# Moving the weight-sum transfer chains of an attention and two feed-forward stages out of the attention, with a shorter ring of weight buffers

## The chip, the cores and the metric

One core of one Trainium2 chip. The metric is device time in microseconds (us) of one execution. Of the kernel before there are three runs: 1626.64, 1627.64 and 1628.63 us.

## What is computed

```python
def reference(**kwargs):
    attn_out = _attn_ref(**attn_kwargs)          # 2 x 8 heads, 768 x 64; scores masked to equal cluster
    B, H, S, D = attn_out.shape
    x = np.ascontiguousarray(attn_out.transpose(0, 2, 1, 3)).reshape(B * S, H * D)
    x = _moe_ref(x=x, **moe_kwargs)              # softplus(x @ w_in) @ w_out, 512 -> 2048 -> 512
    return _moe2_ref(x=x, **moe2_kwargs)         # 8 experts: out += P[:, e] * (relu(x @ w1[e]) @ w2[e])
```

`P` comes from a gate, an exponential and eight rounds of normalising rows and columns. There are 1536 tokens in two batches of 768.

## The kernel before

The program has three stages on one core. **Attention** walks through eight pairs of heads; for each it loads q, k and v, splits each float32 operand into a rounded high part and a low part (`HL`), finds the cluster of each row (`sm`, `tp`, `A`, `OH`), copies rows into the score operands by DMA (`AT`, `Bt`, lines 372 and 451), and does scores (`s`, line 498), exponentials (`E`), transposes (`t`, line 538), the split of the transposed tile (`eh` on ACT, `el` on DVE, line 545) and the product with v (`av`). **The first feed-forward stage** has 16 entries (eight chunks of the hidden width, two batches, list `m1`), each of seven steps; its weights arrive as 64-bit numbers (`r`, lines 139 and 143), are turned into float32 by DVE (`to32`, lines 123 to 127) and split (`wh`, `wl`, `w2h`, `w2l`). **The expert stage** has 16 blocks `k` (two batches, eight experts), each of two layers (`l1_group`, line 910; `l2_piece`, line 945) that use a Strassen-like scheme with seven products in place of eight.

That scheme needs sums of quarters of each expert's two weight matrices. They don't depend on the data, so DMA makes them: `t_step` runs a **chain** of ten transfers for one matrix. A quarter is loaded into a buffer `ts` (SP's queue, line 209), others are added onto it by a transfer that accumulates (POOL's queue, line 207), and the four sums T1 to T4 are written to DRAM (`td`, line 198). Each transfer waits for the one before it:

```python
    STEPS = ("B11", "+B12", "T1", "+B22", "T2", "+B21", "T4", "B12", "+B22", "T3")
```

A transfer that must wait holds up all that stands behind it on its queue: SP issues nearly all other loads and the copies of the attention, POOL also does subtractions and the cluster work. There are 16 chains (`JOBS`, eight experts, two matrices). `JA` and `JF` say where they run: the first four in the attention (one buffer), six in the first feed-forward stage (two buffers), six in the expert blocks (one buffer, one chain per block). Their place is given as a planned time: `at` in the attention, `tsum_at` by feed-forward entry and step, `do` in the expert blocks (28 units of time per block, list `ev2`). A tracing scheduler then makes each engine's order from these times, the priorities and the dependences; `behind_pe` only ties a step's place in that order to TensorE's.

Other names: `W2R` is a ring of four buffers for the second expert matrix (line 856), `w2_load` fills it, `w2_split` splits it on ACT (`vh`) and POOL (`vl`, line 868). `w1_split` splits the first expert matrix in chunks A and B (low part on DVE, line 840) and C (POOL). `xc_prep` (line 968) makes the sums S1 to S4 of the second batch's input (`xS`, lines 72 and 74) and splits seven operands (`chA`, `clA`, `chS`, `clS`, line 990) in the last four groups of steps of block 7. `sinkhorn` is the normalising of `P`, two phases per round, on DVE with a small product `cp` on TensorE.

Of the kernel before, what the change touches and what calls it, by code (L numbers as in the profile page):

```python
# [20 lines left out]
def attention_moe_moe2(ctx, tc, v, qt, kt, centroids, w_in, w_out, w_gate, w1, w2, eye, out, dbg=None):  # L21
# [169 lines left out]
    def t_step(pool, m, e, n):  # L191
        what = STEPS[n]
        if n == 0:
            TS[m, e] = slot_pool[pool].tile([P, 1024], F32, tag="ts", name=f"ts{m}_{e}", bufs=TSB[pool])
        t, w = TS[m, e], what.lstrip("+")
# [25 lines left out]

    TSB = {"ap": 1, "fp": 2, "gp": 1}
    JOBS = [(m, e) for e in range(E) for m in range(2)]
    JA, JF = 4, 10

# [374 lines left out]
    for n in range(4):  # L600
        at(175 + n * 5, lambda n=n: x_split("1_0", first_blk, n), ("xs", 0))
    for j, job in enumerate(JOBS[:JA]):
        for n in range(10):
            at(22 + 42 * j + 4.1 * n, lambda job=job, n=n: behind_pe(t_step, "ap", *job, n), ("tl", 0))
    KEEP = {'sp2': 1, 'fr': 0, 'av': 1, 'am3': 1, 'tpa': 1, 'smc': 0, 'm0': 1, 'rw': 1, 'pz': 1, 'e1': 1}
# [227 lines left out]
    def w1_split(k, u, ch):  # L833
        h, l = T = w1_tiles(ch, 0, f"m{k}_{u}")
        n = 0
        for src in WR[u % 2, ch]:
            m = src.shape[1]
            hs = h[:, n : n + m, :]
            nc.scalar.copy(hs, src)
            (nc.gpsimd if ch == "C" else nc.vector).tensor_tensor(l[:, n : n + m, :], src, hs.bitcast(F32), ALU.subtract)  # L840
            n += m
        W1U.setdefault((k, u), {}).update(w1_use({ch: T}))
# [11 lines left out]
    def w2_load(k, i):  # L854
        name, e = PROD[i][1], k % E
        dst = W2R[(7 * k + i) % 4]
        if name[0] == "B":
# [6 lines left out]
    def w2_split(k, i, p):  # L864
        src = W2R[(7 * k + i) % 4][:, 2 * p : 2 * p + 2, :]
        h, l = (gp.tile([P, 2, DM // 2], F32R, tag=f"v{t}", name=f"v{t}{k}_{i}{p}", bufs=4) for t in "hl")
        nc.scalar.copy(h, src)  # L867
        nc.gpsimd.tensor_tensor(l, src, h.bitcast(F32), ALU.subtract)  # L868
        WH[k, i, p] = h, l
# [97 lines left out]
    def xc_prep(sb, step):  # L967
# [9 lines left out]
        def add(name):  # L977
# [3 lines left out]
            else:  # L981
                tag = {"S1": "A22", "S2": "A12", "S3": "A21"}[name]
                t = gp.tile([P, 2, FH], F32, tag="X" + tag, name=f"x{name}{key}", bufs=XB[tag])
# [3 lines left out]
        def split(name):  # L987
            hi, lo = XC[key, name] = tiles(name)
            nc.scalar.copy(hi, blk[name])
            (nc.gpsimd if name == "A22" else nc.vector).tensor_tensor(lo, blk[name], hi.bitcast(F32), ALU.subtract)  # L990

        for name in (("A11",), ("A12",), (), ("+S1", "+S2", "S2"), ("S1", "+S3", "S3"), ("+S4", "S4"), ("A22",))[step]:
            (add if name[0] == "+" else split)(name.lstrip("+"))
# [11 lines left out]
    for k in range(NB):  # L1005
        for u in range(4):
# [6 lines left out]
            for i in range(7):  # L1013
                do(t0 + i, l1_group, k, u, i)
                if k == E - 1 and u == 3:
                    do(t0 + i + 0.9, xc_prep, 1, i)
        S0 = t1[k] + G1
# [11 lines left out]
        for i in range(7):  # L1029
            b, i_ = divmod(7 * k + i - 4, 7)  # L1030
            do(split_at[b][2 * i_ + 1] + 0.15 if b >= 0 else -1, w2_load, k, i)
# [6 lines left out]
    for j, job in enumerate(JOBS[JF:]):  # L1038
        for n in range(10):
            do(G1 * (j + 1) - 22 + 2.75 * n, behind_pe, t_step, "gp", *job, n)  # L1040
    for hf in range(2):
        do(0.5 + hf, lambda hf=hf: gate(1, hf))
        do(2.5 + 1.5 * hf, lambda hf=hf: gate_max(hf))
    for it in range(8):
        for ph in range(2):
            do(5.5 + 4 * it + 2.5 * ph, lambda it=it, ph=ph: sinkhorn(it, ph))

    tsum_at = {}
    for j, job in enumerate(JOBS[JA:JF]):
        for n in range(10):  # L1050
            tsum_at.setdefault(divmod(1 + int(14.5 * (j // 2 * 2) + 10 * (j % 2) + 2.85 * n), 7), []).append(
                lambda job=job, n=n: behind_pe(t_step, "fp", *job, n)
            )
# [78 lines left out]
```

## Time and profile before

| | |
|---|---|
| profiled execution | 1626.69 us, of which the span of its instructions is 1624.9 us |
| median of the three runs | 1627.64 us |
| TensorE (PE) busy | 1527.6 us, 94% of the span |
| VectorE (DVE) busy | 1257.0 us, 77% |
| ScalarE (ACT) busy | 1005.4 us, 62% |
| GpSimd (POOL) busy | 706.5 us, 43% |
| mean granted TensorE clock | 0.975 of full speed |
| attention | 0 to about 317.5 us |
| first feed-forward stage | about 317.5 to 610 us |
| expert blocks 0 to 7 (first batch) | about 613 to 1108 us |
| expert blocks 8 to 15 (second batch) | to the end |

A stage's engine that is busy without gaps sets that stage's time; an engine's idle time matters only where another waits for it. The stage limits above are the first matmuls of lines 654 and 910 in the trace.

### The profile page before, as it was taken

How to read it: one execution, taken by the hardware profiler on the slowest of the kernel's cores; microseconds unless marked ns; L12 is line 12 of the kernel's file. 1: busy time of each engine (PE TensorE's matmuls, PEld its weight loads, DVE VectorE, ACT ScalarE, POOL GpSimd, SP SyncE). 2: the span in 40 equal slices, each digit the busy share in tenths (PEclk: the TensorE clock that was granted, in tenths of full speed). 3: DMA queues.
4: the chain of work that ended last, by engine and by line, in shares of the span. 5: the costliest groups of instructions: out<-in, count | busy, mean ns of one | idle time of the engine just before them, and what ended most of it. 6: DMA issues, size and time to landing. Idle time of an engine off the chain costs nothing. (4 is left out here: it accounts for less than half of the span.)

```text
span 1624.9 us, 26977 instructions
## 1 busy us (share of the span) xinstructions
PE 1527.6 (94%) x9873; PEld 1449.9 (89%) x9873; DVE 1257.0 (77%) x1836; ACT 1005.4 (62%) x1854; POOL 706.5 (43%) x536
## 2 busy tenths in 40 slices
PE   5888889989999999899999999998999999999998
PEld 4777778879999977799999999998999999999998
DVE  4879779886666266878888888798878878878877
ACT  4767768766665544565665665665566666566663
POOL 3333333432323122355555555555455454445544
PEclk8989989989999999999999999999999999999999
DMA  7678776479888305767788775334443434433421
GB/s 221 167 182 214 183 167 154 98 176 252 212 222 213 101 14 137 190 182 213 202 208 212 205 206 159 121 100 120 145 129 121 124 120 127 124 121 120 125 74 66
DMA packets 268533, 253.02 MB, mean 156 GB/s; under 512 B 12272, under 2 KB 235632, under 8 KB 268400
## 3 DMA queue, kind: packets, MB, share of 16 engines
q1 hardware_dynamic: 242656, 217.67, 44.2%
q0 software_dynamic: 25600, 33.56, 13.3%
q8 instruction: 77, 1.26, 0.3%
q14 instruction: 56, 0.46, 0.1%
q10 hardware_dynamic: 144, 0.07, 0.0%
HBM read 194.10 MB, written 36.70 MB: 142 GB/s over the span
## 5 line engine op out<-in xcount | busy, mean ns | idle before, releaser
L868 POOL TENSOR_TENSOR vl<-w2r,vh 128x512 fp32r<-128x512 f32 x224 | 359.2, 1608 | 410.7 <-ACT vh L867 402.3
L889 DVE TENSOR_TENSOR gl<-XA,gh 128x768 fp32r<-128x768 f32 x160 | 180.2, 1126 | 79.0 <-ACT gh L888 79.0
L888 ACT CAST gh<-XA 128x768 fp32r<-128x768 f32 x160 | 133.9, 837 | 106.9 <-PE Ya1m L945 92.9
L207 POOL DMA_DIRECT2D ts<-in_moe_w_dram x64 | 80.8, 1270 | 193.0 <-DMA ts<-in_moe_w_dram 74.0
L945 PE MATMUL Ya0m<-vh,gl 128*128 128x256 f32 x512 | 144.3, 282 | 0.4 <-DVE gl L889 0.4
L945 PE MATMUL Ya0m<-vh,gh 128*128 128x256 f32 x512 | 144.1, 281 | 0.0
L945 PE MATMUL Ya0m<-vl,gh 128*128 128x256 f32 x512 | 144.1, 281 | 0.0
L867 ACT CAST vh<-w2r 128x512 fp32r<-128x512 f32 x224 | 137.6, 615 | 9.6 <-PE y L688 6.3
L545 DVE TENSOR_TENSOR el<-t,eh 128x384 fp32r<-128x384 f32 x192 | 102.2, 549 | 29.1 <-ACT eh L541 27.6
L541 ACT CAST eh<-t 128x384 fp32r<-128x384 f32 x192 | 90.7, 479 | 37.6 <-PE t L538 24.6
L945 PE MATMUL Yb0m<-vl,gh 128*128 128x256 f32 x384 | 109.5, 285 | 2.6 <-POOL vl L868 2.6
L506 DVE TENSOR_REDUCE sc<-s 128x1 f32<-128x768 f32 x96 | 91.2, 951 | 26.8 <-PE s L498 26.4
L538 PE MATMUL t<-idf,E 128*128 128x128 f32 x576 | 100.6, 284 | 11.9 <-DVE el L545 9.9
L945 PE MATMUL Yb0m<-vh,gh 128*128 128x256 f32 x384 | 109.2, 284 | 2.4 <-DVE x L963 2.4
L945 PE MATMUL Yb0m<-vh,gl 128*128 128x256 f32 x384 | 109.6, 285 | 1.9 <-DVE gl L889 1.9
L931 ACT ACTIVATE XA<-XA 128x768 f32<-128x768 f32 x96 | 81.3, 847 | 41.4 <-DVE XA L929 41.4
L945 PEld LDWEIGHTS Ya0m<-vh,gl 128*128 128x128 f32 x512 | 97.1, 190 | 0.6 <-DVE gl L889 0.6
L945 PEld LDWEIGHTS Ya0m<-vh,gh 128*128 128x128 f32 x512 | 96.9, 189 | 0.0
L945 PEld LDWEIGHTS Ya0m<-vl,gh 128*128 128x128 f32 x512 | 96.9, 189 | 0.0
L511 ACT ACTIVATE E<-s,sc 128x768 f32<-128x768 f32 x96 | 87.0, 906 | 15.4 <-DVE sc L506 14.1
L538 PEld LDWEIGHTS t<-idf,E 128*128 128x128 f32 x576 | 74.8, 146 | 23.7 <-DVE el L545 13.4
L72 DVE TENSOR_TENSOR XS<-XA,XA 128x768 f32<-128x768 f32 x32 | 62.4, 1949 | 33.4 <-ACT XA L927 33.4
(246 smaller groups left out, 5293.1 us busy)
## 6 DMA issues: line engine op xcount, KB each, us to landing
ts<-in_moe_w_dram POOLq DMA_DIRECT2D x64, 512.0 KB, 7.1
td<-ts SPq DMA_DIRECT2D x64, 512.0 KB, 3.6
w2r<-td SPq DMA_DIRECT2D x64, 512.0 KB, 4.0
w2r<-in_moe_w_dram SPq DMA_DIRECT2D x48, 512.0 KB, 3.7
ts<-in_moe_w_dram SPq DMA_DIRECT2D x32, 512.0 KB, 4.8
wf<-td SPq DMA_DIRECT2D x64, 256.0 KB, 3.5
w1r<-td SPq DMA_DIRECT2D x64, 256.0 KB, 3.2
AT<-HL SPq DMA_DIRECT2D x64, 192.0 KB, 4.9
```

The source lines that it names most:

```text
L207: nc.gpsimd.dma_start(t, src, accum_op=ALU.add)
L506: nc.vector.tensor_reduce(SC[i][:, 0, j, t : t + 1], Et[i, t][:, :, 0:CB], AX.XY, ALU.max, negate=True)
L511: nc.scalar.activation(e.rearrange("p (a c) -> p a c", a=2), Et[i, t][:, :, 0:CB], AF.Exp, bias=sc[:, 0, j, t : t + 1], scale=1.0, accum_o ...
L538: nc.tensor.transpose(pt[:, t * P : (t + 1) * P], Et[i, t][:, s * P : (s + 1) * P], idf)
L541: nc.scalar.copy(eh, TT[i, s])
L545: nc.vector.tensor_tensor(el, TT.pop((i, s)), EHL[i, s].bitcast(F32), ALU.subtract)
L867: nc.scalar.copy(h, src)
L868: nc.gpsimd.tensor_tensor(l, src, h.bitcast(F32), ALU.subtract)
L888: nc.scalar.copy(h, src)
L889: nc.vector.tensor_tensor(l, src, h.bitcast(F32), ALU.subtract)
L931: nc.scalar.activation(t, t, AF.Relu, scale=1.0 if name == "A11" else -1.0)
L945: nc.tensor.matmul(ps, g[:, v, ts], w[:, v, :], start=i in (0, 1, 3) and p == 0 and v == 0 and n == 0 and t != 1, stop=p == 1 and v == 1 a ...
```

## The change

- No chain runs in the attention any more. The first feed-forward stage holds eight chains (first step at 1 + 10.3 j of its 112 steps, one transfer each 3.2 steps) in three buffers. Before it held six, in pairs, one transfer each 2.85 steps.
- The expert blocks hold eight chains in place of six, each 22 units after the last with 4.4 units between its transfers (before: 28 and 2.75), so that two run at a time. They take turns between one `ts` buffer and the fourth buffer of `W2R`; the ring of `W2R` for its own loads falls from four to three.
- In block 0, `w1_split` makes the low parts of chunks A and B on POOL, not on DVE.
- `xc_prep` makes the sums S1, S2 and S3 at 14, 17 and 20.4 units of block 7, in buffers of other tags, and the low parts of A11 and S3 on POOL.
- The rounds of `sinkhorn` are 4.2 units apart (before 4), their phases 2.9 (before 2.5).

```diff
         if n == 0:
-            TS[m, e] = slot_pool[pool].tile([P, 1024], F32, tag="ts", name=f"ts{m}_{e}", bufs=TSB[pool])
+            if pool == "wp":
+                TS[m, e] = W2R[3].rearrange("p u d -> p (u d)")
+            else:
+                TS[m, e] = slot_pool[pool].tile([P, 1024], F32, tag="ts", name=f"ts{m}_{e}", bufs=TSB[pool])
...
-    TSB = {"ap": 1, "fp": 2, "gp": 1}
+    TSB = {"fp": 3, "gp": 1}
...
-    JA, JF = 4, 10
+    JF = 8
...
-    for j, job in enumerate(JOBS[:JA]):
-        for n in range(10):
-            at(22 + 42 * j + 4.1 * n, lambda job=job, n=n: behind_pe(t_step, "ap", *job, n), ("tl", 0))
...
-            (nc.gpsimd if ch == "C" else nc.vector).tensor_tensor(l[:, n : n + m, :], src, hs.bitcast(F32), ALU.subtract)
+            (nc.gpsimd if ch == "C" or k == 0 else nc.vector).tensor_tensor(l[:, n : n + m, :], src, hs.bitcast(F32), ALU.subtract)
...
-        dst = W2R[(7 * k + i) % 4]
+        dst = W2R[(7 * k + i) % 3]
...
-                tag = {"S1": "A22", "S2": "A12", "S3": "A21"}[name]
+                tag = {"S1": "A21", "S2": "A12", "S3": "A22"}[name]
...
-            (nc.gpsimd if name == "A22" else nc.vector).tensor_tensor(lo, blk[name], hi.bitcast(F32), ALU.subtract)
+            (nc.gpsimd if name in ("A11", "S3", "A22") else nc.vector).tensor_tensor(
+                lo, blk[name], hi.bitcast(F32), ALU.subtract
+            )
...
-                    do(t0 + i + 0.9, xc_prep, 1, i)
+                    do(t0 + i + 0.9, xc_prep, 1, (PROD[i][0],) if i != 2 else ("S2", "+S4"))
+        if k == E - 1:
+            for name, d in (("+S1", 14), ("+S2", 17), ("+S3", 20.4)):
+                do(t1[k] + d, xc_prep, 1, (name,))
...
-            b, i_ = divmod(7 * k + i - 4, 7)
+            b, i_ = divmod(7 * k + i - 3, 7)
...
-            do(G1 * (j + 1) - 22 + 2.75 * n, behind_pe, t_step, "gp", *job, n)
+            do(2 + 22 * j + 4.4 * n, behind_pe, t_step, ("gp", "wp")[j % 2], *job, n)
...
-            do(5.5 + 4 * it + 2.5 * ph, lambda it=it, ph=ph: sinkhorn(it, ph))
+            do(5.5 + 4.2 * it + 2.9 * ph, lambda it=it, ph=ph: sinkhorn(it, ph))
...
-    for j, job in enumerate(JOBS[JA:JF]):
+    for j, job in enumerate(JOBS[:JF]):
...
-            tsum_at.setdefault(divmod(1 + int(14.5 * (j // 2 * 2) + 10 * (j % 2) + 2.85 * n), 7), []).append(
+            tsum_at.setdefault(divmod(1 + int(10.3 * j + 3.2 * n), 7), []).append(
```

Three places show what moves. The first is SP's queue in the attention, between the loads for head pairs 6 and 7; `td1_0` and `ts1_0` belong to the chain of expert 0's second matrix, `Bt4..`, `AT5..` to head pairs 4 and 5. Before:

```order
L341 DMA rT16_2166<-in_kt_dram 128x768
L198 DMA td1_0_82<-ts1_0_1560 128x4x256
L451 DMA Bt400_1576<-OHT4_1878 16x768
L451 DMA Bt411_1627<-OHT4_1878 16x768
L143 DMA r210_0_1_3968<-in_moe_w_out_dram 128x512
L198 DMA td1_0_82<-ts1_0_1560 128x4x256
L372 DMA AT500_2041<-HL05_1788 64x768 x2
L209 DMA ts1_0_1560<-in_moe2_w2_dram 128x4x256
L341 DMA rT07_2642<-in_qt_dram 128x768
```

And now:

```order
L344 DMA rT16_2146<-in_kt_dram 128x768
L454 DMA Bt400_1563<-OHT4_1862 16x768
L454 DMA Bt411_1614<-OHT4_1862 16x768
L375 DMA AT500_2022<-HL05_1773 64x768 x2
L344 DMA rT07_2616<-in_qt_dram 128x768
L143 DMA r210_0_1_3924<-in_moe_w_out_dram 128x512
```

The chain's stores, which wait for an accumulating transfer, no longer stand ahead of the copies of `Bt` and `AT`.

The second place is SP's queue in the first feed-forward stage, from the weights of chunk 5 to those of chunk 6 (`r110_0_5` and `r210_0_5`, then `r110_0_6`). Before:

```order
L143 DMA r210_0_5_5280<-in_moe_w_out_dram 128x512 x2
L209 DMA ts1_3_4888<-in_moe2_w2_dram 128x4x256
L198 DMA td0_3_77<-ts0_3_4695 128x2x512
L198 DMA td1_3_85<-ts1_3_4888 128x4x256
L139 DMA r110_0_6_5616<-in_moe_w_in_dram 128x4x128 x2
```

And now:

```order
L143 DMA r210_0_5_5247<-in_moe_w_out_dram 128x512 x2
L201 DMA td1_1_83<-ts1_1_4655 128x4x256
L201 DMA td1_0_82<-ts1_0_4168 128x4x256
L201 DMA td0_1_75<-ts0_1_4421 128x2x512
L212 DMA ts0_2_4939<-in_moe2_w1_dram 128x2x512
L212 DMA ts0_1_4421<-in_moe2_w1_dram 128x2x512
L201 DMA td1_1_83<-ts1_1_4655 128x4x256
L139 DMA r110_0_6_5586<-in_moe_w_in_dram 128x4x128 x2
```

Six transfers of three chains stand ahead of the weights of chunk 6, where three of two chains stood.

The third place is POOL's order at the start of expert block 0 (`vl0_..` are splits of the second matrix, `wlCm0_1` and the like those of the first in the block's second group). Before:

```order
L868 TENSOR_TENSOR vl0_11_7160<-w2r0_6689,vh0_11_7159 128x512
L840 TENSOR_TENSOR wlCm0_1_6826<-w1r3_6694,whCm0_1_6825 128x256
L840 TENSOR_TENSOR wlCm0_1_6826<-w1r2_6693,whCm0_1_6825 128x512
L207 DMA ts0_5_6814<-in_moe2_w1_dram 128x2x512
L840 TENSOR_TENSOR wlCm0_2_6928<-wf_71,whCm0_2_6927 128x768
```

And now:

```order
L868 TENSOR_TENSOR vl0_11_7130<-w2r0_6667,vh0_11_7129 128x512
L840 TENSOR_TENSOR wlAm0_1_6734<-w1r0_6669,whAm0_1_6733 128x512
L840 TENSOR_TENSOR wlBm0_1_6767<-w1r1_6670,whBm0_1_6766 128x512
L210 DMA ts0_4_6731<-in_moe2_w1_dram 128x2x512
L840 TENSOR_TENSOR wlCm0_1_6804<-w1r3_6672,whCm0_1_6803 128x256
L840 TENSOR_TENSOR wlCm0_1_6804<-w1r2_6671,whCm0_1_6803 128x512
L840 TENSOR_TENSOR wlAm0_2_6833<-wf_71,whAm0_2_6832 128x512
L840 TENSOR_TENSOR wlBm0_2_6865<-wf_71,whBm0_2_6864 128x512
L840 TENSOR_TENSOR wlCm0_2_6905<-wf_71,whCm0_2_6904 128x768
```

Two subtractions of 128x512 per group have come over from DVE, and an accumulating transfer stands among them as before.

## Rows read from the trace of the kernel before

**Rows 1.** Busy time by stretch: stretch, its length, PE, PEld, DVE, ACT, POOL; clock, DMA share, GB/s
```profile
66.00:317.50 251.50, 216.51 (x1317) 192.20 (x1315) 210.86 (x375) 186.48 (x411) 88.99 (x90) 0.94 0.72 170
317.50:364.00 46.50, 39.53 (x195) 35.20 (x196) 41.40 (x58) 27.95 (x59) 20.77 (x14) 0.89 0.63 159
364.00:545.00 181.00, 179.51 (x1026) 167.50 (x1025) 113.71 (x193) 111.82 (x218) 55.37 (x42) 1.00 0.84 217
...
582.00:700.00 118.00, 106.62 (x567) 91.12 (x566) 82.42 (x153) 55.63 (x101) 37.06 (x28) 0.93 0.52 128
700.00:1080.00 380.00, 374.53 (x2622) 368.86 (x2621) 310.71 (x393) 234.28 (x397) 204.27 (x144) 1.00 0.68 184
1080.00:1120.00 40.00, 33.37 (x227) 32.47 (x226) 39.97 (x42) 24.79 (x40) 26.94 (x13) 0.91 0.32 99
```

**Rows 2.** Waits of SP's queue, 66 to 317.5 us: total, times, longest
```profile
SPq L198 <- DMA ts<-in_moe_w_dram: 87.2, 14, 11.0
```

**Rows 3.** Timeline of SP, ACT, DVE and PE around 185 us: start, duration, instruction, idle before
```profile
175.23 0.37 SPq L198 DMA_DIRECT2D td<-ts  x1
...
185.34 0.84 ACT L356 ACTIVATE HL<-rT 128x768 fp32r<-128x768 f32 x1 [5.83 <-DMA Bt<-HL]
...
186.58 0.56 DVE L545 TENSOR_TENSOR el<-t,eh 128x384 fp32r<-128x384 f32 x1 [6.22 <-ACT eh L541]
...
187.20 0.90 PE L538 MATMUL t<-idf,E 128*128 128x128 f32 x3 [5.64 <-DVE el L545]
```

**Rows 4.** Waits of PE, 66 to 317.5 us
```profile
PE t L538 <- DVE el L545: 9.9, 8, 5.6
PE po L440 <- POOL OH L433: 5.8, 5, 2.4
...
PE s L498 <- DMA Bt<-OHT: 3.5, 2, 2.0
```

**Rows 5.** Busy time by stretch within the attention, columns as in rows 1
```profile
35.00:68.00 33.00, 29.39 (x193) 26.67 (x192) 27.34 (x50) 27.30 (x62) 8.32 (x9) 1.00 0.59 173
66.00:246.00 180.00, 150.97 (x899) 133.88 (x898) 146.82 (x262) 128.78 (x283) 61.39 (x63) 0.91 0.77 185
246.00:317.50 71.50, 65.54 (x420) 58.31 (x418) 64.04 (x114) 57.70 (x129) 27.61 (x27) 1.00 0.58 132
```

**Rows 6.** DMA queues: packets, MB, share of 16 engines over the span
```profile
q1 hardware_dynamic: 242656, 217.67, 44.2%
q0 software_dynamic: 25600, 33.56, 13.3%
```

**Rows 7.** Waits of ACT, 317.5 to 560 us
```profile
ACT cm L123 <- DMA r<-in_moe_w_in_dram: 5.0, 2, 2.7
ACT whCm L839 <- DMA wf<-td: 4.5, 1, 4.5
```

**Rows 8.** Groups of DVE, then of POOL, 545 to 700 us: count, busy, mean ns, idle before
```profile
L840 DVE TENSOR_TENSOR wlAm<-w1r,whAm 128x512 fp32r<-128x512 f32 x4 | 2.7, 680 | 0.0
...
L840 POOL TENSOR_TENSOR wlCm<-w1r,whCm 128x512 fp32r<-128x512 f32 x3 | 4.3, 1447 | 0.3 <-ACT whCm L839 0.2
```

**Rows 9.** Waits of PE, 620 to 720 us
```profile
PE cp L761 <- DVE cs L757: 4.4, 3, 3.5
```

**Rows 10.** Timeline of POOL and DVE around 1105 us
```profile
1102.01 5.59 POOL L868 TENSOR_TENSOR vl<-w2r,vh 128x512 fp32r<-128x512 f32 x3
...
1100.28 2.59 DVE L72 TENSOR_TENSOR XS<-XA,XA 128x768 f32<-128x768 f32 x1
...
1109.13 0.94 DVE L72 TENSOR_TENSOR XA<-XA,XA 128x768 f32<-128x768 f32 x1
```

**Rows 11.** Groups of DVE and waits of PE, 1080 to 1120 us
```profile
L72 DVE TENSOR_TENSOR xS<-x 128x768 f32<-128x768 f32 x2 | 3.5, 1778 | 0.0
...
PE Yb0m L945 <- POOL vl L868: 2.6, 1, 2.6
...
PE Yb0m L945 <- DVE gl L889: 1.9, 1, 1.9
```

More of the change, by code (lines that the diff above doesn't have):

```diff
@@ L864, in w2_split @@
     def w2_split(k, i, p):
-        src = W2R[(7 * k + i) % 4][:, 2 * p : 2 * p + 2, :]
+        src = W2R[(7 * k + i) % 3][:, 2 * p : 2 * p + 2, :]
         h, l = (gp.tile([P, 2, DM // 2], F32R, tag=f"v{t}", name=f"v{t}{k}_{i}{p}", bufs=4) for t in "hl")
@@ L989, in split @@
             nc.scalar.copy(hi, blk[name])
-            (nc.gpsimd if name == "A22" else nc.vector).tensor_tensor(lo, blk[name], hi.bitcast(F32), ALU.subtract)
-        for name in (("A11",), ("A12",), (), ("+S1", "+S2", "S2"), ("S1", "+S3", "S3"), ("+S4", "S4"), ("A22",))[step]:
+            (nc.gpsimd if name in ("A11", "S3", "A22") else nc.vector).tensor_tensor(
+                lo, blk[name], hi.bitcast(F32), ALU.subtract
+            )
+        for name in step:
             (add if name[0] == "+" else split)(name.lstrip("+"))
```

## The prediction

> **What bounds the kernel now.** I read the busy times by stretch first [rows 1]. From 364 to 545 us, in the first feed-forward stage, PE is busy 179.5 of 181 us, and from 700 to 1080 us, in the expert blocks, 374.5 of 380 us, both at a granted clock of 1.00 of 2.4 GHz: there the matmuls are the time. Four stretches are different. In the attention, 66 to 317.5 us, PE is idle for 35.0 us and its clock stands at 0.94; at the entry to the feed-forward stage, 317.5 to 364, it is idle for 7.0 us at 0.89; where the expert blocks begin, 582 to 700, for 11.4 us at 0.93; where the second batch begins, 1080 to 1120, for 6.6 us at 0.91, with DVE busy 39.97 of 40 us. Only there can a change of order give time back. A clock below 1.00 means that part of the stretch ran at 1.2 GHz, so it holds a second loss beside the idle time: 0.06 x 251.5 = 15 us of full-speed time in the attention, 5, 8 and 4 us in the others. It follows the gaps, so it shrinks if they do.
>
> The waits tell why the attention has gaps. SP's queue waited 87.2 us there for an accumulating transfer, in 14 waits of up to 11.0 us, before it could issue a chain's store [rows 2]. The timeline shows what that does [rows 3]: a store goes out at 175.23, the copies of AT and Bt queued behind it follow only then, ACT then waits 5.83 us for the last of an earlier copy before it may overwrite HL, DVE waits 6.22 us behind ACT, and PE stands still for 5.64 us. Of the waits of PE [rows 4], those for el (9.9 us, of which this one is 5.6), for OH from POOL's queue (5.8) and for the Bt copies (3.5) can come from there.
>
> **The change, part by part.** I add to the profiled execution, 1626.69 us; the median of the runs, 1627.64, is 0.95 us above it.
>
> *The chains leave the attention.* Four chains go, 16 accumulating transfers on POOL's queue and 24 others on SP's. No row shows the attention without them, so I bound the gain by how densely DVE, the busiest engine after PE, works. DVE does 146.82 us of work from 66 to 246 us, a share of 0.816 [rows 5]. The stretch from 246 to 317.5, with a lighter DMA load (0.58 for 0.77) and a clock of 1.00, reaches 64.04 / 71.5 = 0.896. At that share the 180 us would be 146.82 / 0.896 = 163.9, so 16.1 less. The other end is the stretch from 35 to 68 us, before the first chain, which reaches only 27.34 / 33 = 0.83 and would give 180 - 146.82 / 0.83 = 3.1. I take 12: nearer to the upper end, because that stretch does the same work later in the same stage, and the waits that I can trace to transfers (5.6 + 5.8 + 3.5 = 14.9 us) are of that size. Ends: -16 and -3.
>
> *Eight chains in the feed-forward stage.* 64 accumulating transfers took 13.3% of 1624.9 us of all DMA engines, so 3.4 us each; the other queue moved 217.67 MB in 44.2%, so a plain transfer of 0.524 MB takes 1.7 us [rows 6]. A chain is 4 x 3.4 + 6 x 1.7 = 23.9 us of the 16 engines. Up to 545 us the stage uses 0.63 x 46.5 + 0.84 x 181 = 181 us [rows 1]; two more chains make 229. The stage lasts until about 582, so 264.5 us, and the DMA engines would be at 0.87 on average, little above the 0.84 at which PE loses nothing now. So the transfers fit, and the lower end is no loss. The danger is order: six transfers of three chains stand ahead of a chunk's weights on SP's queue where three of two stood. ACT already waits for weights, 5.0 us in two waits of up to 2.7, and 4.5 us once for the first expert block's [rows 7]; ACT works in order, so the activations queue behind such a wait. If each of six chunks waits 3 us, near the 2.7, and all of it reaches PE, that is 18 us. I take +3, one wait, because PE ran without gaps from 364 to 545 with waits of 2 to 3 us on ACT. Ends: 0 and +18.
>
> *The first expert block.* Eight subtractions of 128x512 leave DVE, 8 x 0.68 = 5.4 us [rows 8]; on POOL each takes 1.45, in all 11.6 us. POOL is busy 37.1 of 118 us there [rows 1], so it has room. The wider spacing of the normalising rounds lets DVE finish before PE gets to cp, for which PE waited 4.4 us [rows 9]. I take -4, that wait and little else. The upper end of the gain is most of the 11.4 us of idle time, 10.
>
> Against it speaks that DVE and POOL hold each other up. While POOL ran three subtractions, 1102.01 to 1107.6, and the one before them, a DVE sum of 128x768 took 2.59 us; when POOL was idle, at 1109.13, the same kind took 0.94 [rows 10]. If a subtraction on POOL stops DVE for its whole length, the move costs DVE up to 11.6 and returns 5.4, so +6. That is the end on the other side. The Trainium skill has this as a rule (SBUF — State Buffer, section "Who interferes with whom"): a DVE instruction with two inputs in SBUF and a GpSimd instruction that reads SBUF use one shared read interface, and the later one is blocked until the earlier has finished. By that rule the term would be +6, not -4; the trace agrees in kind (2.59 for 0.94), but DVE did go on between POOL's instructions, so not every one of them costs its full length.
>
> *The ring of three and the chains in pairs.* From 700 to 1080 us PE idles 5.5 us in all [rows 1], so there is little to gain. Chains have 4.4 units for each transfer, some 9.5 us of a block of about 61 (61 x 4.4 / 28), against 6.0 before, so POOL and SP should wait for them less; the two added chains add 2 x 23.9 us of DMA time to a stretch at 0.68. A load into the ring waits for the split three loads earlier, not four. I take 0, ends -4 and +6.
>
> *The second batch's sums.* DVE is never idle from 1080 to 1120, and two of its sums there (3.5 us) as well as two low parts now elsewhere [rows 11] are work that PE waits behind. Two of three sums go to block 7's middle, two low parts to POOL. Of PE's 6.6 us of idle time, 1.9 was behind a DVE split, but 2.6 was behind POOL's vl, which gets two more subtractions ahead of it. With half a slow-clock stretch (2 us) I take -5. Ends: -10, all of the idle time and the clock, and +2, if vl comes later by one more subtraction.
>
> **Sum:** -12 + 3 - 4 + 0 - 5 = -18 on 1626.69 gives 1608.7, and on the scale of the median 1609.6.
>
> **The rivals.**
>
> 1. *All the slack comes back.* The attention gains 16, the weights are never late, the starts of the batches gain 9 each and the blocks 1: -35, so 1593. For it: the slow clock (15 us in the attention alone) goes with the gaps. Against it: DVE at 0.9 has never been exceeded over a long stretch. Chance 0.13.
> 2. *The attention is bound by its own chain of dependences*, as from 35 to 68 us without any chain: it gains 3, the rest as forecast: -9, so 1618.6. Chance 0.17.
> 3. *DVE and POOL hold each other up* in the first expert block: +6 for -4 there, the rest as forecast: -8, so 1619.6. By the rule named above this is the outcome; the chance that I give it follows from how incompletely the rows show it. Chance 0.12.
> 4. *The feed-forward stage becomes bound by its weights*: slower than before. SP's queue serves three chains in turn, and whenever an accumulating transfer is late (the longest wait now is 11.0 us [rows 2]), the next weights are late too. The other terms sum to -21, so it decides from 3 us on PE per chunk over seven chunks; at 4.5 us, the length of ACT's longest wait now [rows 7], it costs 31 and gives 1637. For it: the DMA engines are near full and the queue is longer. Against it: chunks 2 to 4 have fewer chain steps ahead of them than the later ones, and each chain now has more time per transfer. Chance 0.13.
>
> **How the numbers follow.** The forecast has 0.45. It and rivals 1 to 3 hold 0.87; the range takes them in with the bounds of the small terms, 1591 to 1629, and leaves out rival 4 and the far end of rival 1. A measurement of this kernel can tell about 0.2%, 3.3 us, from no change. Faster than that are the forecast, rivals 1 and 2 and most of 3: 0.80. Within it lie the poor ends of rivals 2 and 3: 0.07. Slower is rival 4: 0.13.
>
> **What would show it.** In the profile of the changed kernel: the attention ends near 305 us instead of 317.5, with SP's long waits for the accumulating transfer gone there and PE's 5.64 us gap as well; DMA share from 66 to 300 us falls to about 0.4, and from there to 545 rises to 0.9; ACT's waits for weights in the feed-forward stage stay under 15 us and PE stays at 97% or more; from the end of that stage PE's idle time in the first 118 us falls under 8; around the start of the second batch it falls under 3. The forecast is wrong if the attention shrinks by less than 6 us, if PE idles over 12 us in the middle of the feed-forward stage, or if DVE's time in the first expert block grows though eight instructions left it.

## The result, and the profile after

The changed kernel takes 1612.88 us (median of four runs, 1606.54 to 1614.02); the kernel before, in four runs beside it, 1628.01 us (1626.64 to 1628.63). The ratio is 0.990, 95% interval 0.9873 to 0.9927: faster by 15.1 us, where 1609.6 was forecast. The profiled run took 1613.91 us with a span of 1612.1, 12.8 us less than the span before, at a mean granted clock of 0.979 (before 0.975). Where these 12.8 us come from is not what the prediction said.

Busy time by stretch of the changed kernel (columns as in [rows 1]; the limits are those of its own stages):

```profile
66.00:289.30 223.30, 206.00 (x1329) 185.05 (x1328) 205.88 (x377) 187.76 (x416) 69.84 (x74) 0.99 0.39 99
289.30:336.00 46.70, 41.77 (x211) 37.99 (x212) 42.93 (x64) 30.10 (x61) 21.51 (x14) 0.89 0.66 175
336.00:517.00 181.00, 169.76 (x943) 157.56 (x941) 107.47 (x178) 98.92 (x193) 58.83 (x45) 0.97 0.98 247
...
690.00:1066.00 376.00, 368.02 (x2557) 362.81 (x2556) 304.61 (x386) 231.40 (x390) 213.11 (x148) 0.99 0.78 210
1066.00:1106.00 40.00, 33.82 (x233) 32.81 (x232) 38.31 (x39) 25.50 (x42) 28.89 (x16) 0.96 0.32 100
```

The attention ends at 289.3 us, not 317.6. DVE, the densest engine after PE, is busy 205.88 of 223.3 us there, 0.92, PE's clock is 0.99 and the DMA share 0.39. The middle of the feed-forward stage has the DMA engines at 0.98, and PE, idle for 1.5 us in 181 before [rows 1], now idles 11.2.

All stages in us, for the kernels e1 to e12 that follow, too. The attention ends with the first matmul of line 654, the feed-forward stage with the first of line 910. The expert blocks are cut by the count of line 910's matmuls, 168 to a block: the first two blocks, the next five, two more (into the second batch), and the rest up to the last matmul.

| | attention ends | feed-forward stage | first blocks | next five blocks | into the second batch | rest |
|---|---|---|---|---|---|---|
| before | 317.6 | 295.7 | 113.3 | 306.7 | 132.6 | 454.6 |
| changed | 289.3 | 313.0 | 107.7 | 311.1 | 132.0 | 454.6 |
| difference | -28.3 | +17.3 | -5.6 | +4.4 | -0.6 | 0 |
| e1 lows on DVE | 288.1 | 295.3 | 107.9 | 311.4 | 132.7 | 454.6 |
| e2 six and ten chains | 290.7 | 291.6 | 110.2 | 326.2 | 134.4 | 453.2 |
| e3 first block's lows back on DVE | 287.4 | 308.5 | 107.1 | 313.0 | 132.7 | 453.1 |
| e4 second batch's sums as before | 289.5 | 308.5 | 110.1 | 311.8 | 132.9 | 454.9 |
| e5 plain loads added | 319.6 | 310.0 | 108.9 | 312.7 | 132.8 | 453.0 |
| e6 before, chains on POOL's queue | 322.4 | 291.9 | 109.6 | 306.7 | 132.5 | 454.5 |
| e7 normalising rounds as before | 287.8 | 314.0 | 106.8 | 311.1 | 132.7 | 453.0 |
| e8 all lows on DVE | 289.3 | 296.4 | 106.1 | 311.2 | 132.7 | 453.1 |
| e9 full copies added | 295.7 | 308.9 | 109.6 | 308.2 | 132.8 | 453.1 |
| e10 tiny copies added | 296.0 | 315.5 | 108.2 | 313.1 | 132.8 | 454.5 |
| e11 nine and seven chains | 289.0 | 312.2 | 107.8 | 303.9 | 131.9 | 455.1 |
| e12 before, narrow adds | 299.6 | 294.1 | 110.4 | 308.6 | 132.5 | 454.6 |

Two large terms, -28.3 and +17.3, cancel in part. The table also shows how far a stage scatters where nothing in it was edited: the attention by 3.3 us (e1 to e4, e7, e8, e11 and the changed kernel), the feed-forward stage of the changed kernel from 308.5 to 315.5, the first blocks of the kernel before's code from 109.6 to 113.3 (e6, e12, before). Each row is one profiled execution; that of e10 was the slowest of its ten (1626.77 us, median 1617.49).

**The attention.** SP's waits there, total, times, longest:

```profile
SPq L454 <- ACT eh L544: 59.2, 5, 20.3
SPq L344 <- POOL HL L368: 37.6, 8, 7.6
```

The 87.2 us for the accumulating transfer [rows 2] are gone. What SP waits for now is computing work: it waits 59.2 us before copies of `Bt` (line 454) and 37.6 before loads of q and k (line 344), whose buffer POOL's `HL` still reads. So its wait is the work's own pace. PE's idle time from 66 us to the stage's end falls from 35.1 to 17.3 us and its busy time from 216.5 to 206.0 for the same matmuls: 17.8 us of gaps, and 10.5 us of longer matmuls, at a clock of 0.94 before and 0.99 now.

**The feed-forward stage.** Waits of DVE, ACT and SP from 289 to 545 us:

```profile
DVE wf L125 <- POOL wlBD L255: 21.5, 4, 7.3
...
ACT cm L123 <- DVE wf L125: 23.5, 9, 7.5
...
ACT whCm L839 <- DMA wf<-td: 8.6, 1, 8.6
...
ACT cm L123 <- DMA r<-in_moe_w_in_dram: 5.5, 2, 3.3
...
SPq L201 <- DMA ts<-in_moe_w_dram: 85.1, 20, 11.1
```

Before, from 317 to 545 us, the first of these lines was

```profile
DVE wf L125 <- POOL wlBD L252: 3.9, 4, 3.1
```

What grew most on DVE and ACT is not a wait for a transfer that brings weights: DVE waits for POOL's low part `wlBD`, and ACT for DVE. PE's waits for the activation `gf` grew with them, from 9.9 us in 7 waits to 22.2 in 10. The timeline of one of DVE's four waits shows the chain (start, duration, instruction, idle before and its releaser):

```profile
398.53 1.30 POOL L210 DMA_DIRECT2D ts<-in_moe_w_dram  x1 [8.53 <-DMA td<-ts]
...
399.35 1.77 POOL L255 TENSOR_TENSOR wlBD<-wf,whBD 128x512 fp32r<-128x512 f32 x1
401.16 0.43 DVE L125 TENSOR_SCALAR wf<-cm 128x512 int32<-128x512 int32 x1 [7.33 <-POOL wlBD L255]
...
402.70 0.55 DVE L668 SCALAR_TENSOR_TENSOR gf<-p,u 128x384 f32<-128x384 f32 x1
...
403.28 0.51 ACT L670 CAST gh<-gf 128x384 fp32r<-128x384 f32 x1 [1.00 <-DVE gf L668]
...
403.30 0.69 PE L654 MATMUL p<-chA,whBD 128*128 128x384 f32 x1 [4.88 <-DVE gf L668]
```

Read it from above. POOL stood 8.53 us at an accumulating transfer whose chain's store had not landed. Behind it in POOL's order stood the subtraction `wlBD`, the last reader of the weight buffer `wf`. DVE, which was to write the next weights into `wf`, waited 7.33 us, and the activation `gf`, which needed nothing of all this, stood behind it on DVE. PE stood still for 4.88 us. At 518 us there is a second kind, and this one is a late load: the first expert block's chunk C, whose load stood on SP behind three chain stores (9.3 us) and a wait of 4.9 us for POOL's low part `wlA`.

```profile
517.86 0.83 ACT L839 CAST whCm<-wf 128x768 fp32r<-128x768 f32 x1 [8.59 <-DMA wf<-td]
...
520.84 0.45 PE L654 MATMUL p<-chA,whA 128*128 128x384 f32 x1 [4.31 <-DVE gf L668]
```

**The expert blocks.** PE's wait for the sum `XA` in the five blocks from 710 us is 7.2 us in four waits (5.0 before). One of them in POOL's and DVE's timeline:

```profile
862.71 1.20 POOL L210 DMA_DIRECT2D ts<-in_moe_w_dram  x1
...
863.47 1.78 POOL L210 DMA_DIRECT2D w2r<-in_moe_w_dram  x1
...
864.06 5.13 DVE L72 TENSOR_TENSOR XS<-XA,XA 128x768 f32<-128x768 f32 x1 [2.45 <-ACT XA L927]
...
864.26 2.85 POOL L840 TENSOR_TENSOR wlCm<-wf,whCm 128x768 fp32r<-128x768 f32 x1
...
866.08 2.28 POOL L868 TENSOR_TENSOR vl<-w2r,vh 128x512 fp32r<-128x512 f32 x1
...
873.43 0.69 PE L910 MATMUL l3m<-chS,whBm 128*128 128x384 f32 x1 [2.88 <-DVE XA L929]
```

The steps of two chains issue together on POOL, its subtractions then run back to back, and the DVE sum beside them takes 5.13 us, where the same kind took 0.94 alone and 2.59 beside POOL [rows 10]. PE's longest wait, 2.88 us, comes behind it. DVE as a whole is no busier in these blocks than before (252.8 us in both): the 20 sums of this kind took 33.5 us for 28.7, but the 70 low parts `gl` 76.2 for 82.4.

### The profile page after: what moved, and what is told of

It reads as the page before. It is cut to its first block, busy times and chain, and to the rows that moved or that the text cites. A ratio compares the mean times of both kernels' runs of the same rounds, so it can differ in the third digit from the quotient of the medians.

```text
span 1612.1 us, 26967 instructions
## 1 busy us (share of the span) xinstructions
PE 1518.6 (94%) x9873; PEld 1442.9 (90%) x9873; DVE 1244.7 (77%) x1826; ACT 1006.5 (62%) x1854; POOL 725.5 (45%) x546
## 5 line engine op out<-in xcount | busy, mean ns | idle before, releaser
L889 DVE TENSOR_TENSOR gl<-XA,gh 128x768 fp32r<-128x768 f32 x160 | 175.4, 1096 | 81.9 <-ACT gh L888 81.8
L888 ACT CAST gh<-XA 128x768 fp32r<-128x768 f32 x160 | 134.1, 838 | 108.9 <-PE Ya1m L945 94.5
L867 ACT CAST vh<-w2r 128x512 fp32r<-128x512 f32 x224 | 137.7, 615 | 10.3 <-PE y L688 6.7
L210 POOL DMA_DIRECT2D ts<-in_moe_w_dram x48 | 61.9, 1330 | 108.6 <-DMA ts<-in_moe_w_dram 33.9
L514 ACT ACTIVATE E<-s,sc 128x768 f32<-128x768 f32 x96 | 87.2, 909 | 14.7 <-DVE sc L509 13.6
```

The lines of the kernel that those rows point to most:

```text
L514: nc.scalar.activation(e.rearrange("p (a c) -> p a c", a=2), Et[i, t][:, :, 0:CB], AF.Exp, bias=sc[:, 0, j, t : t + 1], scale=1.0, accum_o ...
L889: nc.vector.tensor_tensor(l, src, h.bitcast(F32), ALU.subtract)
```

## The experiments

Three questions were open: by what way the attention gained more than twice the forecast (the theories were the waits at the head of a queue, the load on the DMA engines, and the order that the planner chooses), what the feed-forward stage lost (POOL's queue or late loads), and whether the small edits did anything. Ratios are to the kernel before in the same set of runs.

### e1: the low parts of the feed-forward stage's first matrix on DVE

```diff
-            (nc.vector if u == (1, 0, 0, 0) else nc.gpsimd).tensor_tensor(l, src, h.bitcast(F32), ALU.subtract)
+            nc.vector.tensor_tensor(l, src, h.bitcast(F32), ALU.subtract)
```

> The changed kernel with the low parts of the first matrix in the feed-forward stage (wlA, wlBD, line 255) made by DVE and not by POOL. In the changed kernel the stage from its first matmul to that of the expert blocks takes 313.0 us, before 295.7. Theory POOL (the buffer wf comes free late because its subtraction stands on POOL's queue behind an accumulating transfer; DVE then waits 21.5 us for it and the activations behind it): DVE's wait for wlBD is gone, PE's gaps of 4.9 and 3.3 us go, the stage falls by 8 to 14 us, the time to about 1602. Theory DMA (the 16 engines are at 0.98 there and weights land late): the stage stays within 3 us of 313, since ACT's waits only change their name from the buffer to the landing; time 1610 to 1615.

Measured: 1597.31 us (1591.30 to 1600.25), ratio 0.9814, interval 0.9784 to 0.9844. The stage takes 295.3 us for 313.0, at the same chains and the same transfers:

```profile
288.10:583.40 295.30, 279.56 (x1558) 253.93 (x1559) 186.55 (x308) 169.99 (x333) 82.95 (x59) 0.99 0.78 200
```

and of DVE's and ACT's waits up to 545 us there stay

```profile
DVE w2f L125 <- POOL w2l L259: 10.0, 3, 4.1
...
ACT cm L123 <- DMA r<-in_moe_w_in_dram: 5.8, 1, 5.8
ACT whCm L839 <- DMA wf<-td: 5.3, 1, 5.3
```

The waits for loads are still there (5.8 and 5.3 us); the wait behind `wlBD` is gone, PE's waits for `gf` from 336 us on are 11.2 us, and the stage takes what it took before (295.7), more than the 8 to 14 us expected. So the loss went through POOL's queue and the buffer, and DVE had room for the subtractions.

### e2: six chains in the feed-forward stage as before, ten in the expert blocks

```diff
-    JF = 8
+    JF = 6
...
-            do(2 + 22 * j + 4.4 * n, behind_pe, t_step, ("gp", "wp")[j % 2], *job, n)
+            do(2 + 18 * j + 3.9 * n, behind_pe, t_step, ("gp", "wp")[j % 2], *job, n)
...
-            tsum_at.setdefault(divmod(1 + int(10.3 * j + 3.2 * n), 7), []).append(
+            tsum_at.setdefault(divmod(1 + int(14.5 * (j // 2 * 2) + 10 * (j % 2) + 2.85 * n), 7), []).append(
```

> The changed kernel with six chains in the feed-forward stage at the places of before (pairs, 2.85 steps per transfer) and ten in the expert blocks (each 18 units after the last, 3.9 units per transfer). Both theories of the stage expect it to fall from 313.0 us to 297 +- 3, as it has the chains of before; what it tells is whether the loss comes from the two added chains at all, or from what else moved. The first seven expert blocks carry 25% more transfers than in the changed kernel: if DMA load is what costs there (311 us from block 1's end to block 6's end against 307 before), they lose another 4 us; if it is the order on POOL, within 2 us. Time 1598 to 1602.

Measured: 1612.91 us, ratio 0.9916 (0.9886 to 0.9946), no better than the change, where 1598 to 1602 was expected. The feed-forward stage is back at 291.6 us, but the five blocks take 326.2, 15 more, which neither of the two expectations for them (within 2 us, or another 4) had. POOL's and PE's waits there:

```profile
POOL w2r L210 <- DMA w2r<-in_moe_w_dram: 24.0, 4, 6.5
POOL ts L210 <- DMA ts<-in_moe_w_dram: 8.9, 3, 4.3
```

```profile
PE l3m L910 <- DVE XA L929: 12.8, 6, 3.9
PE l0m L910 <- DVE XA L929: 5.7, 2, 4.1
```

POOL waits 32.9 us there for accumulating transfers before it issues the next; in the changed kernel it waits 5.6 us at these steps, for other transfers. PE waits 18.5 us for `XA` in place of 7.2. So chains moved can cost again where they go. Ten chains also stand closer here (18 units for 22, 3.9 for 4.4), and the run doesn't tell their number from their distance.

### e3, e4 and e7: the small edits undone, one at a time

e3 puts the low parts of block 0's chunks A and B back on DVE:

```diff
-            (nc.gpsimd if ch == "C" or k == 0 else nc.vector).tensor_tensor(l[:, n : n + m, :], src, hs.bitcast(F32), ALU.subtract)
+            (nc.gpsimd if ch == "C" else nc.vector).tensor_tensor(l[:, n : n + m, :], src, hs.bitcast(F32), ALU.subtract)
```

> The changed kernel with the low parts of chunks A and B of block 0 back on DVE. If that part gave the 5.6 us that the first two blocks won (113.3 to 107.7 us), the time rises by 4 to 6 us and the blocks go back to 112. If DVE and POOL hold each other up, so that the move gives nothing or costs, the time stays or falls by up to 6 us.

Measured: 1608.38 us, ratio 0.9893 (0.9868 to 0.9918); first blocks 107.1 us for 107.7. The moved subtractions neither gave nor cost anything that can be told from the scatter.

e4 puts the tags, engines and places of `xc_prep` back as they were before:

> The changed kernel with the second batch's sums and splits (xc_prep) as before: all at the end of block 7, all low parts but one on DVE. The stretch of the last block of the first batch and the first of the second took 132.6 us before and 132.0 in the changed kernel. My forecast of a gain of 5 expects 4 to 5 us more here; that the work only changed place on an engine that is busy anyway expects a difference of less than 1.5 us.

Measured: 1612.05 us, ratio 0.9912 (0.9883 to 0.9940); into the second batch 132.9 us for 132.0. The moved sums are worth less than 1 us.

e7 puts the normalising rounds back at their old distance:

```diff
-            do(5.5 + 4.2 * it + 2.9 * ph, lambda it=it, ph=ph: sinkhorn(it, ph))
+            do(5.5 + 4 * it + 2.5 * ph, lambda it=it, ph=ph: sinkhorn(it, ph))
```

> The changed kernel with the normalising rounds at their old distance (4 and 2.5 units). The moved subtractions did not shorten the first expert blocks, so if the distance of the rounds did, they take 112 to 114 us here for the 107.7 of the changed kernel, and the wait of PE for cp is back at about 4 us. If it was the chains' new places (none in the first blocks' middle), they stay at 107 to 108.

Measured: 1610.16 us, ratio 0.9909 (0.9881 to 0.9936); first blocks 106.8 us. PE's waits there:

```profile
PE l3m L910 <- DVE XA L929: 3.3, 3, 1.4
PE cp L761 <- DVE cs L757: 2.2, 3, 0.9
```

In the changed kernel the wait for `cp` is 0.7 us, before, 4.4 [rows 9]. So the wider distance does shorten that wait, by 1.5 us of the 3.7, but the stage doesn't show it. Neither of the two edits, undone alone, takes back the 5.6 us of the first blocks; they were not undone together, and the chains' new places were not tested by themselves. So the 5.6 us have no shown cause; and part of them is scatter, since the old code of these blocks took 109.6 to 113.3 us (before, e6, e12) and the new one, whole or with one edit undone, 106.1 to 110.1.

### e5: plain loads in the attention

```diff
+    def fill(n):
+        t = slot_pool["ap"].tile([P, 2, 512], F32, tag="fill", name=f"fill{n}", bufs=2)
+        nc.sync.dma_start(t, w1[n % E, 0 : DM // 2, (n // E) % 2 * 512 : (n // E) % 2 * 512 + 512].rearrange("(k p) f -> p k f", p=P))
+
+    for n in range(56):
+        at(22 + 3.0 * n, lambda n=n: behind_pe(fill, n), ("tl", 0))
```

> The changed kernel with 56 plain loads of 0.5 MB added on SP's queue in the attention (about 56 x 1.7 = 95 us of the DMA engines, as much as the four chains took), into two buffers that nobody reads: the load without the chain's waits. Theory (the attention of before was held up by stores and accumulating transfers that waited at the head of SP's and POOL's queues): the attention still ends near 289 us, at most 294, and the run stays within 5 us of the changed kernel. Rival (the transfers' load on the DMA engines was what cost the 28 us): the attention ends at 305 us or later.

Measured: 1643.85 us, ratio 1.0115 (1.0091 to 1.0139). The attention ends at 319.6: by the text on record the load theory wins. But the run doesn't tell them apart, as SP's waits show:

```profile
SPq L607 <- DMA fill<-in_moe_w_dram: 57.9, 27, 4.8
```

The loads take turns in two buffers, and each waits at the head of SP's queue for the one two before it. The planner also gave PE another order. So this run has the load, waits and an order of its own at once; e9, e10 and e12 take them apart.

### e6: the attention's chains on POOL's queue alone, in the kernel before

```diff
-            nc.sync.dma_start(TD[m][e][TORD.index(w)].rearrange("k p f -> p k f"), t)
+            (nc.gpsimd if pool == "ap" else nc.sync).dma_start(TD[m][e][TORD.index(w)].rearrange("k p f -> p k f"), t)
...
-            nc.sync.dma_start(t, src)
+            (nc.gpsimd if pool == "ap" else nc.sync).dma_start(t, src)
```

> The kernel before, with the four chains of the attention kept but all their transfers issued from POOL's queue, so that SP never waits for an accumulating transfer and POOL waits for every step. Theory of the changed kernel's gain as SP's queue alone: the attention ends near 290 us instead of 317.6. If it was POOL's queue, where the cluster work stands behind the chain: it ends at 317 us or later. If both: between, near 303. The later stages are those of before.

Measured: 1625.81 us, ratio 1.0007 (0.9989 to 1.0025). The attention ends at 322.4, which by the text on record points to POOL's queue. SP no longer waits for a chain before the attention's copies (one wait, 39.7 us for the feed-forward stage's first chain, comes after the last copy, at 275 us); POOL does, and PE for the cluster work behind it:

```profile
POOL td L198 <- DMA ts<-in_moe_w_dram: 70.5, 15, 6.9
POOL ts L207 <- DMA ts<-in_moe_w_dram: 27.3, 8, 6.9
```

```profile
PE po L440 <- POOL OH L433: 16.5, 5, 8.5
```

Taking the wait off one queue and putting it on another gives nothing. `po` waited 5.8 us for POOL before [rows 4], now 16.5. But POOL waits 125.1 us at the chains' steps here, for 64.2 before, so the run doesn't say how much SP's queue alone cost; e12 says more on that.

### e9 and e10: the load without the waits, and the order without the load

In place of e5's buffers, a copy from DRAM to DRAM that waits for nothing (e9), and the same with 8 columns (e10); the loop that places them is e5's:

```diff
...
+    def fill(n):
+        nc.sync.dma_start(FILL[n], w1[n % E, 0 : DM // 2, (n // E) % 2 * 512 : (n // E) % 2 * 512 + 512])
...
```

```diff
...
+    def fill(n):
+        nc.sync.dma_start(FILL[n, :, 0:8], w1[n % E, 0 : DM // 2, (n // E) % 2 * 512 : (n // E) % 2 * 512 + 512][:, 0:8])
...
```

> The plain loads into two buffers gave the attention its old length back, but SP still waited for a buffer at each of them (57.9 us) and the planner gave the engines another order. Here the 56 transfers are copies of the same 0.5 MB from DRAM to DRAM, which wait for nothing: the load alone. Load theory: the attention ends at 305 us or later, and the transfers of q, k, v, AT and Bt land later than in the changed kernel (7.0 for 3.2, 6.2 for 3.8 us with the plain loads). Queue theory (only a wait at the head of SP's queue costs): at most 294.

> The same 56 copies at the same places of SP's queue, but of 8 columns each (16 KB): the order of the engines is that of the run with the full copies to within 18 of the first 1300 rows of PE, and the load on the DMA engines is gone. Load theory and queue theory both expect an attention that ends at 288 to 294 us. If it ends at 305 or later, it was the order that the planner chose around the added transfers (the third theory) which cost the time in the run with the plain loads, and perhaps in the kernel before.

Measured: e9 1613.75 us, ratio 0.9912 (0.9884 to 0.9940); e10 1617.49 us, ratio 0.9947 (0.9921 to 0.9973). The attention ends at 295.7 and 296.0. The attention in e9, and its transfers of 90 to 280 us (KB each, median us from issue to landing):

```profile
66.00:295.70 229.70, 209.44 (x1329) 187.82 (x1328) 207.69 (x377) 187.81 (x416) 69.07 (x74) 0.98 0.80 223
```

```profile
AT<-HL SPq DMA_DIRECT2D x40, 192.0 KB, 6.3
...
rT<-in_qt_dram SPq DMA_DIRECT2D x3, 384.0 KB, 7.7
```

and in e10:

```profile
66.00:296.00 230.00, 207.29 (x1328) 185.97 (x1326) 209.36 (x377) 187.68 (x416) 69.27 (x74) 0.99 0.40 95
```

```profile
AT<-HL SPq DMA_DIRECT2D x40, 192.0 KB, 3.9
...
rT<-in_qt_dram SPq DMA_DIRECT2D x3, 384.0 KB, 3.0
```

Twice the load, 0.80 for 0.40, and landings of 6.3 us in place of 3.9, change the stage by 0.3 us, and the median with the full copies is not the slower one: the copies are issued early enough. The load theory falls, for a load of plain copies. Beside e9, e5 speaks for the waits: the same 56 transfers of 0.5 MB, with 57.9 us of waits at the head of SP's queue, end the attention 23.9 us later, though in another order. Both e9 and e10 end 6 to 7 us after the changed kernel, and both missed their 294: what they share is 56 more transfers on SP and the order that the planner chose around them. Which of the two it was isn't separated.

### e12: the kernel before with narrow adds

```diff
+        if what[0] == "+" and pool == "ap":
+            t, src = t[:, :, 0:8], src[:, :, 0:8]
```

> The kernel before with its four chains in the attention, but each accumulating transfer there adds only 8 of the columns, so it lands sooner and SP's stores behind it wait less; the other transfers, their places and nearly the whole order of the engines (32 of PE's first 900 rows differ) are those of before. Left out: the greater part of the sums of four chains. Wait theory (the wait at the head of SP's queue for the accumulating transfer is what the attention lost): SP's 87.2 us fall below 50 and the attention ends at 305 us or earlier, for 317.6. Order theory (what cost was the order that the planner chose with the chains in it): it ends at 312 us or later. Between the two, each has a part.

Measured: 1605.26 us, ratio 0.9881 (0.9856 to 0.9907). The attention ends at 299.6 us for 317.6, and

```profile
SPq L198 <- DMA ts<-in_moe_w_dram: 49.1, 13, 11.0
...
PE po L442 <- POOL OH L435: 7.9, 5, 3.6
...
PE t L540 <- DVE el L547: 2.6, 9, 0.5
```

```profile
66.00:299.60 233.60, 209.33 (x1311) 187.37 (x1309) 205.07 (x373) 185.37 (x408) 89.23 (x90) 0.96 0.59 147
```

With all four chains in place, 38 us less of waiting on SP give back 18.0 of the 28.3 us. `t`'s wait for `el` on PE, of which the prediction had traced 5.6 us to SP's copies, falls from 9.9 to 2.6 us, and the one for the `Bt` copies (3.5 before [rows 4]) is gone; its wait for POOL's `OH` doesn't fall (5.8 before, 7.9 here), though POOL too waits less at the chains' steps (64.2 us before, 47.1 here). So the 18.0 us point to SP's queue rather than to POOL's. The lighter load (0.59 for 0.72) isn't the cause, if what e9 shows for plain copies holds for it. The other 10.3 us may lie in the 49.1 us of waits that are left or in the order; the runs don't divide them.

### e8 and e11: versions meant to beat both

e8 is e1 with the low part `w2l` (line 259) on DVE too, and e3's edit.

> A version meant to beat both: the changed kernel with all low parts of the feed-forward stage's weights on DVE, so that none stands behind an accumulating transfer on POOL's queue, and with the first block's subtractions back on DVE. Theory (POOL's queue holds the weights' buffers): the feed-forward stage takes 290 to 295 us for 313.0, the wait of 10.0 us on the second matrix's low part goes as well, and the run is near 1595. Rival (DVE becomes the late engine, 32 more subtractions of 0.7 us on it): the stage takes 297 us or more.

Measured: 1595.44 us (1592.08 to 1598.23), ratio 0.9813 (0.9782 to 0.9844), as e1: the stage takes 296.4 us, between the two expectations, so neither is shown. No wait of DVE for POOL is left up to 545 us, but ACT waits 14.2 us there for the first matrix's weights (5.8 in e1), and PE idles 14.8 us in the stage for e1's 15.7.

e11 is e1 with nine and seven chains:

```diff
-    JF = 8
+    JF = 9
...
-            do(2 + 22 * j + 4.4 * n, behind_pe, t_step, ("gp", "wp")[j % 2], *job, n)
+            do(14 + 22 * j + 4.4 * n, behind_pe, t_step, ("gp", "wp")[j % 2], *job, n)
...
-            tsum_at.setdefault(divmod(1 + int(10.3 * j + 3.2 * n), 7), []).append(
+            tsum_at.setdefault(divmod(1 + int(9.8 * j + 3.2 * n), 7), []).append(
```

> A version meant to beat both: the first experiment's kernel (the feed-forward stage's low parts on DVE) with nine chains in that stage and seven in the expert blocks, for the DMA share in the stage's last 67 us is only 0.18 there. If the stage has room, it stays at 295 us and the expert blocks win about 1.5 us (a sixth of the 10 us by which five blocks exceed 5 x 60.1): 1594 to 1597. Rival (the DMA engines, at 1.01 in the stage's middle, have no room): the stage takes 300 us or more, and the run about 1601.

Measured: 1607.13 us, ratio 0.9887 (0.9866 to 0.9907). The five blocks win 7.5 us over e1, five times the estimate, and the feed-forward stage loses 16.9. The rival's 300 us and 1601 are passed, too. Its timeline:

```profile
503.17 0.49 SPq L828 DMA_DIRECT2D wf<-td  x1
```

```profile
516.46 0.83 ACT L839 CAST whCm<-wf 128x768 fp32r<-128x768 f32 x1 [17.95 <-DMA wf<-td]
...
518.30 0.56 DVE L668 SCALAR_TENSOR_TENSOR gf<-p,u 128x384 f32<-128x384 f32 x1 [20.25 <-ACT u L667]
...
518.91 0.69 PE L654 MATMUL p<-chA,whA 128*128 128x384 f32 x1 [14.68 <-DVE gf L668]
```

Here the weights are late, as in the prediction's fourth rival, though most of the delay is not on SP's queue: a load of 0.26 MB goes out at 503.17, nearly 5 us after ACT began to wait for it, and lands some 13 us later, with the DMA engines at 1.02 from 336 to 517 us; ACT waits 17.95 us, with the activations behind it, and PE stands 14.68 us in one piece.

## Why the prediction was right, and where it was not

The total fell inside the range and 3.3 us from the forecast, and faster was right. The sum, -18 for a measured -12.8 of span and -15.1 of median, was close because two terms were mis-sized in opposite directions, by 16.3 and 14.3 us. That they cancel is luck: nothing in the prediction ties one to the other.

- **The attention, -12 (ends -16 and -3): -28.3.** The mechanism, waits at the head of SP's queue, is shown for 18.0 of the 28.3 us (e12), and the load was rightly not blamed (e9). The step that failed was the bound: the share 0.896 of [rows 5] was taken from 246 to 317.5 us, a stretch that itself had five of the sixteen accumulating transfers in it, as the densest that this work could be. Without chains DVE reaches 0.92 over 223 us. At that share the first 180 us alone would give 20.8 us and the stretch that served as the bound 2.0 more; the last 5.5 us come from DVE's own busy time, which fell from 210.9 to 205.9 us for the same work. Seen from PE, the clock was named ("it follows the gaps, so it shrinks if they do", 15 us) and then left out of the term: 10.5 of the 28.3 us are PE's shorter busy time. The result lies well outside the ends; rival 2, an attention bound by its own dependences, is excluded.
- **The feed-forward stage, +3 (ends 0 and +18): +17.3.** The end was right, the way was not. The prediction looked at weights late behind chains on SP and at ACT (behind four chains, not three, in the order shown for chunk 6). What was late was POOL's subtraction behind an accumulating transfer, then the buffer, then DVE (e1). The argument "the transfers fit" was true (e1 has the same transfers in 295.3 us) and not enough. The test that it set itself, PE idle for under 12 us in the middle, was met by 0.8 us (11.2), and its 97% was missed (169.76 of 181, 94%), as was its 15 us of ACT's waits for weights (17.4, of which 8.6 at 518 us). Late weights, which rival 4 named, cost PE once in the changed kernel (4.31 us) and fully only in e11 (14.68 us), there mostly by the time to landing.
- **The first expert block, -4: -5.6.** The size is near, the cause given isn't borne out. The wait for `cp` fell from 4.4 to 0.7 us, but with the old distance of the rounds (e7) or with the subtractions back on DVE (e3) the stretch doesn't get longer. Rival 3, with +6, fell too: DVE's busy time fell from 85.7 to 81.6 us in it. Beside e3 (83.5) it fell by 1.9 us, for six subtractions fewer in the stretch, 4.1 us at 0.68 each: a part came back as longer instructions of DVE, but far from +6, and the stretch's time shows none of it. The rule of the Trainium skill behind that rival (SBUF — State Buffer, "Who interferes with whom") isn't refuted by this, since it bears only on instructions that run at the same time; in the later blocks the trace agrees with it, 5.13 us beside POOL's subtractions for 0.94 alone.
- **The ring of three and the chains in pairs, 0 (ends -4 and +6): +4.4.** Inside the ends. "POOL should wait for them less" came true (15.4 us at the chains' steps before, 5.6 now), but where the steps of two chains meet, issues and subtractions stand back to back on POOL, and a DVE sum beside them grew. e2 (+15 with ten chains) and e11 (-7.5 with seven) show that the blocks' time depends on how many chains run there and where. It doesn't simply follow their number: e11's seven, 22 units apart in two buffers with the ring of three, take 303.9 us, 2.8 less than the old six (306.7). So neither the pairs nor the shorter ring must cost.
- **The second batch's sums, -5: -0.6.** The step that failed took PE's idle time there as waiting for the sums. PE still idles 6.2 us of 40 (6.6 before), now 2.9 for `XA` and 2.0 for POOL's `vl`; DVE's relief of 1.7 us found another engine that was late. The undone edit (e4) says the same. The sign for this stretch, PE idle for under 3 us, was missed.

## What to carry to other kernels

A transfer that waits for another transfer is paid for by whatever stands behind it on the queue that issues it, so before placing one, list what follows it on that queue, computing instructions of the engine that owns the queue included, and who needs their buffers; in the attention the share of the DMA engines told nothing of it (0.40 and 0.80 gave the same length), while at 1.02, in e11, a load took 13 us to land. Moving such a chain to a stage "with room" pays in full only if the last reader of a buffer isn't queued behind it there: one engine's name in one line (e1) turned a gain of 1.0% into one of 1.9%. When a bound is taken from a dense stretch of the same profile, make sure that the stretch is free of what is being removed.

## What was not expected of the hardware

- Doubling the DMA share from 0.40 to 0.80 lengthened the `AT` copies' time to landing from 3.9 to 6.3 us, and that of three loads of q from 3.0 to 7.7 (those of k stayed near 3.1), and cost the stage nothing (e9, e10).
- Accumulating transfers of 8 columns still took 4.6 us (8 KB) and 3.0 us (16 KB) from issue to landing, in the median, those of 512 KB 7.8, and SP still waited 49.1 us for them, for 87.2 (e12): the wait is far from proportional to the bytes. By the start of each transfer in the two traces, some 12 of the 49.1 us and 13 of the 87.2 passed before POOL had issued it; of e12's longest wait, 11.0 us, that is 8.0. The rest is mostly the landing.
- A DVE sum of 128x768 took 5.13 us beside POOL's subtractions and transfer issues, over five times its 0.94 us alone.
